# Grouped attention with SwiGLU on one core: who reads the fourth head's scores out of PSUM, and in how many exponentials

## The chip, the cores and the metric

The kernel runs on one core of a Trainium2 chip. The time is device microseconds of one launch, the median of several runs. Instruction times come from one profiled execution. Engines: PE multiplies matrices into PSUM, VectorE (DVE) and ScalarE (ACT) read PSUM and write SBUF, GpSimd (POOL) works on SBUF only, SyncE (SP) issues DMAs.

## The reference, cut to what matters

Two layers, each an attention block and a feed-forward block, with normalised inputs and residual sums. The sequence has 2048 rows of 448; 16 query heads of width 28 share one key and one value head.

```python
def _A_ref(x, wq, wk, wv, wo):
    q = (x @ wq).reshape(B, S, H, Dh).transpose(0, 2, 1, 3)
    k = x @ wk
    v = x @ wv
    scores = einsum("bhqd,bkd->bhqk", q, k) * (Dh ** -0.5)
    o = einsum("bhqk,bkd->bhqd", softmax(scores), v)
    return o.transpose(0, 2, 1, 3).reshape(B, S, H * Dh) @ wo
...
x = x + _A_ref(_layernorm(x), A_wq, A_wk, A_wv, A_wo)
x = x + _B_ref(_layernorm(x), B_w_gate, B_w_up, B_w_down)   # (silu(x @ w_gate) * (x @ w_up)) @ w_down
# and both once more
```

## The kernel before, in words

Every engine runs its instructions in the order in which the program lists them (`manual_schedule`, line 73); semaphores between engines are set by the framework from the tiles that are written and read. So the order of the Python calls is each engine's queue.

**Attention, `scores` (line 565).** Queries are cut into 4 chunks of 512 rows and 4 groups of 4 heads: 16 groups i (`GR`). For each, 16 key tiles of 128 keys are walked through: 256 steps n a layer, two steps to a pair d. `step(n)` (line 595) multiplies key tile kt with the 4 heads of the group. The heads use 32 rows of PE each and run beside each other; three products (high and low parts of the numbers) add up for each head. Heads 0 to 2, the triples, go to `three`, three PSUM banks; there are two such sets, for even and odd steps. Head 3, the single, goes to `one`, one of the two other banks, 6 and 7: `single(n // 2 + n)` (line 572 and 599).

Then come the exponentials (lines 608 to 618). In an even step ScalarE takes the single straight from PSUM (line 616), then the triples (line 617). In an odd step it takes the triples first (line 611); VectorE copies the single to SBUF as `raw` (line 613), and ScalarE takes it from there (line 614).

`pv(d)` (line 640) multiplies the exponentials of a pair's two steps with the values. Its result goes to bank `single(d + 1)`, and VectorE adds it to the group's sums in SBUF (line 657; line 654 copies for a group's first pair). A bank of the singles so holds in turn an even step's single, the product of the pair before, and an odd step's single. The loop that sets the order stands in lines 708 to 733: for an odd n it calls `step(n)`, then `pv(d - 1)`, then `between(d)`, which three times a layer does the output projection of a chunk in the same banks (lines 630 to 638), then what is due of `post`.

`post(i)` (line 661) divides: a DMA takes the row sums (line 668), and `rest`, called three pairs later out of `due`, checks their range and takes reciprocals on VectorE (lines 674 to 676), sends them out and back by two DMAs on SP (lines 678, 679) and multiplies and splits on GpSimd (lines 686, 687). `later` holds the steps of the next normalisation, spread over single n (lines 693 to 706).

**Maxima.** A softmax needs a bound for each query. `diagonal` (line 392) writes `kdiag`, block-diagonal copies of eight keys; `maxima` (line 419) multiplies them with the queries and reduces on VectorE (lines 426 to 435). For the last chunk it runs after step 1 of the stage, in bank 6 (line 724).

**Buffers.** `halves(name)` (line 119) hands out two buffers of 128x1024 in turn, for the group's sums (`o2`), the feed-forward's hidden values (`h2`) and one weight load.

**Feed-forward** (line 751 on) isn't changed; its first unit follows the stage's last `pv` on PE (lines 734 to 737). The branch with `full=True` runs only if a range check fails, which doesn't happen here.

Of the kernel before, what the change touches and what calls it, by code (L numbers as in the profile page):

```python
# [8 lines left out]
F32 = mybir.dt.float32  # L9
F32R = mybir.dt.float32r  # L10
AF = mybir.ActivationFunctionType
# [4 lines left out]
P = 128  # L16
# [11 lines left out]
SCALE = DH ** -0.5  # L28
# [24 lines left out]
def forward(  # L53
# [14 lines left out]
    nc = tc.nc  # L68
# [9 lines left out]
    pers = ctx.enter_context(tc.tile_pool(name="pers", bufs=1))  # L78
# [40 lines left out]
    def halves(name):  # L119

        return pers.tile([P, 2, 512], F32R, tag="halves", name=name, bufs=2)
# [28 lines left out]
    qts = [pers.tile([P, 2, 512], F32R, name=f"qstack{n}") for n in range(2)]  # L150
    qraw = pers.tile([P, 512], F32, name="qraw")
    bottom = pers.tile([4, 32], F32, name="bottom")
    kd, mask = None, None
    if not full:
        kd, mask = pers.tile([P, 4, P], F32R, name="kdiag"), pers.tile([P, 16, 4], F32, name="mask")

    def weights(fc):
        fs = slice(P * fc, P * fc + P)
# [173 lines left out]
    class Attention:  # L332
# [58 lines left out]

        def diagonal(self):

            nc.vector.tensor_tensor(
                kd[0:112].rearrange("p g (n k) -> p (g n) k", k=8),
                self.few[0:112, None, :].to_broadcast([112, 64, 8]),
                mask[0:112].rearrange("p n j -> p (n j)")[:, :, None].to_broadcast([112, 64, 8]),
                ALU.mult,
            )
# [19 lines left out]
        def maxima(self, c, cands=ALL):  # L419


            pm = bank(cands)[1]
            for n, g in enumerate(TURN):
                nc.tensor.matmul(pm, kd[0:112, g, :], self.hi[g], start=(n == 0), stop=(n == 3))  # L424
            side = pers.tile([P, 512], F32, name="sg")
            nc.vector.transpose(side, pm)
            ng = pers.tile([P, 64], F32, name="ng")
            nc.vector.tensor_reduce(ng, side.rearrange("p (n k) -> p n k", k=8), AX.X, ALU.max, negate=True)
            two = pers.tile([P, 4, 2, 16], F32R, name="two")
            hi, lo = two[:, :, 0, :], two[:, :, 1, :]  # L430
            ng = ng.rearrange("p (b j) -> p j b", j=4)
            nc.vector.tensor_copy(hi, ng)
            nc.vector.tensor_tensor(lo, ng, hi, ALU.subtract)
            flat = pers.tile([P, P], F32, name="flat")
            nc.vector.transpose(flat, two.rearrange("p j z b -> p (j z b)").bitcast(F32))
            self.rowsof[c] = dram.tile([P, P], F32, name=f"rows{self.layer}_{c}")
            nc.sync.dma_start(self.rowsof[c], flat)
# [10 lines left out]
        def max_steps(self, i):  # L448

            got = {}  # L450
            q = qts[i % 2]

            def one(j, qt, kc):
                if not got:
                    got["mx"] = pers.tile([P, 16, KC], F32, name="mx", bufs=2)
                n = 4 * j + qt
                pm = self.mbank()[1]
                js, qs = slice(32 * j, 32 * j + 32), slice(P * qt, P * qt + P)
                for n_, (z, k) in enumerate(((0, 0), (1, 0), (0, 1))):
                    nc.tensor.matmul(  # L460
                        pm, q[js, z, qs], keys[kc][js, k, :], start=(n_ == 0), stop=(n_ == 2), tile_position=(32 * j, 0)
                    )
                nc.vector.tensor_reduce(got["mx"][:, n, kc : kc + 1], pm, AX.X, ALU.max)

            def fin():
                got["ng"] = pers.tile([P, 16], F32, name="ng", bufs=2)
                nc.vector.tensor_reduce(got["ng"], got["mx"], AX.X, ALU.max, negate=True)

            def place(pn=None):

                if pn is None:
                    pn = self.mbank()[1]
                nc.tensor.transpose(pn[0:16, 0:P], got["ng"], ident)
                nh = pers.tile([16, P], F32R, name="nh", bufs=2)
                nl = pers.tile([16, P], F32R, name="nl", bufs=2)
                nc.vector.tensor_copy(nh, pn[0:16, 0:P])
                nc.vector.tensor_tensor(nl, pn[0:16, 0:P], nh, ALU.subtract)
                for z, n_ in enumerate((nh, nl)):
                    dma(q[28:125:32, z, :].rearrange("j (t w) -> j t w", w=P), n_)

            order = [(j, qt, kc) for j in range(4) for qt in range(4) for kc in range(KC)]
            if i == 0:
                order.sort(key=lambda o: o[2])
            fs = [lambda o=o: one(*o) for o in order]
            return fs[:-1] + [lambda: (fs[-1](), fin())], place
# [79 lines left out]
        def scores(self, ff):  # L565
            next(switch)
            with tc.tile_pool(name=f"at{self.layer}", bufs=1, reuse_waits="tile") as wp:
                woh = wp.tile([P, NG, D], F32R, name="woh")
                wol = wp.tile([P, NG, D], F32R, name="wol")
                on, accs, pts = {}, {}, {}  # L570
                todo, due = [], {}
# [23 lines left out]
                def step(n):  # L595


                    i, kt = divmod(n, NT)
                    three, one = threes[n % 2], single(n // 2 + n)
                    q, k, ks = qts[i % 2], keys[kt // 4], slice(P * (kt % 4), P * (kt % 4) + P)  # L600
                    for z, (kp, part) in enumerate(((0, 0), (1, 0), (0, 1))):
                        for j in range(4):
                            js = slice(32 * j, 32 * j + 32)
                            nc.tensor.matmul(  # L604
                                three[:, j, :] if j < 3 else one, k[js, kp, ks], q[js, part, :],
                                start=(z == 0), stop=(z == 2), tile_position=(32 * j, 0),
                            )
                    pt = wp.tile([P, 3, 512], F32, name="pt", bufs=3)
                    pt1 = wp.tile([P, 512], F32, name="pt1", bufs=3)
                    if n % 2:  # L610
                        nc.scalar.activation(pt, three, AF.Exp, scale=SCALE)  # L611
                        raw = wp.tile([P, 512], F32, name="raw")
                        nc.vector.tensor_copy(raw, one)  # L613
                        nc.scalar.activation(pt1, raw, AF.Exp, scale=SCALE)  # L614
                    else:
                        nc.scalar.activation(pt1, one, AF.Exp, scale=SCALE)  # L616
                        nc.scalar.activation(pt, three, AF.Exp, scale=SCALE)  # L617
                    pts[n] = [*(pt[:, j, :] for j in range(3)), pt1]

                def between(d):  # L620

# [39 lines left out]
                def post(i):  # L661

                    c, g = GR[i]
                    out2 = accs.pop(i)
                    oraw, rb = out2[:, 0, :], out2[:, 1, :]
                    rs = wp.tile([P, 16], F32, name="rs", bufs=2)
                    for j in range(4):
                        nc.sync.dma_start(rs[32 * j : 32 * j + 32, :], oraw[32 * j + DH : 32 * j + DH + 1, :])

                    def rest():  # L670
                        if fine is not None:
                            under = wp.tile([P, 16], F32, name="under", bufs=2)
                            for bound, op in ((LIMIT, ALU.is_lt), (1.0 / LIMIT, ALU.is_gt)):
                                nc.vector.tensor_scalar(under, rs, bound, None, op)
                                nc.vector.tensor_tensor(fine, fine, under, ALU.mult)
                        nc.vector.reciprocal(rs, rs)
                        rd = dram.tile([4, 512], F32, name="rd", bufs=2)
                        nc.sync.dma_start(rd.rearrange("j (p n) -> (j p) n", n=16), rs)
                        nc.sync.dma_start(rb, rd[:, None, :].to_broadcast([4, 32, 512]))
                        if g == 0:  # L680
                            on[c] = (
                                wp.tile([P, NG, 512], F32R, name="onh"),
                                wp.tile([P, NG, 512], F32R, name="onl"),
                            )
                        oh, ol = on[c]
                        nc.gpsimd.tensor_tensor(rb, oraw, rb, ALU.mult)
                        split(oh[:, g, :], ol[:, g, :], rb)
                        if g == NG - 1 and c < NC - 1:
                            todo.append(c)

                    return rest
# [16 lines left out]
                for n in range(last):  # L708
# [17 lines left out]
                        later.pop(n)()  # L726
                    d, odd = divmod(n, 2)
                    if odd:
                        if d:
                            pv(d - 1)  # L730
                        between(d)
                        if d in due:
                            due.pop(d)()
                pv(last // 2 - 1)
                self.lent = None
                next(switch)
# [292 lines left out]
```

## Time and profile before

| | before |
|---|---|
| median of 3 runs | 1986.77 us (1986.52 to 1987.32) |
| span of the profiled execution, first to last instruction | 1984.8 us |
| mean granted PE clock | 0.999 |
| ScalarE rows in the stages: triples (lines 611 and 617), 256 each | 1454 and 1453 ns |
| ScalarE: single from SBUF (line 614), from PSUM (line 616), 256 each | 622 and 591 ns |
| VectorE: single's copy (line 613), 256; sum's add (line 657), 224 | 692 and 691 ns |
| PE: value matmuls (line 647), 4096 | 598 ns |

Beside its span the profiled execution has no time of its own on record; the median of the runs lies 2.0 us above the span. A row names the line, the engine, what it writes from what, how often, and the mean of one. Rows of a timeline begin with start and duration in us; brackets at the end give the idle time before and what ended it. Instructions on PE, VectorE and ScalarE overlap their neighbours a little, so durations add up to more than the distance of their starts.

### The profile page before, as it was taken

How to read it: one execution, taken by the hardware profiler on the slowest of the kernel's cores; microseconds unless marked ns; L12 is line 12 of the kernel's file. 1: busy time of each engine (PE TensorE's matmuls, PEld its weight loads, DVE VectorE, ACT ScalarE, POOL GpSimd, SP SyncE). 2: the span in 40 equal slices, each digit the busy share in tenths (PEclk: the TensorE clock that was granted, in tenths of full speed). 3: DMA queues.
4: the chain of work that ended last, by engine and by line, in shares of the span. 5: the costliest groups of instructions: out<-in, count | busy, mean ns of one | idle time of the engine just before them, and what ended most of it. 6: DMA issues, size and time to landing. Idle time of an engine off the chain costs nothing. (4 is left out here: it accounts for less than half of the span.)

```text
span 1984.8 us, 44687 instructions
## 1 busy us (share of the span) xinstructions
PE 1969.2 (99%) x18519; PEld 1322.9 (67%) x18519; DVE 812.1 (41%) x1410; ACT 1278.6 (64%) x2140; POOL 528.7 (27%) x571
## 2 busy tenths in 40 slices
PE   9999999999999999999999999999999999999998
PEld 7544545445458999999984444454454789988887
DVE  7444543544434222322554335445454432222222
ACT  4899797997953333333349998979979433333332
POOL 4212111132213233333341221111231232233320
PEclk9999999999999999999999999999999999999999
DMA  5101020121210011100131111102111101011102
GB/s 163 55 23 31 23 51 21 32 58 28 72 33 9 24 32 32 32 24 19 51 107 35 30 31 30 44 12 61 32 55 45 31 17 30 18 31 32 32 1 76
DMA packets 93382, 77.52 MB, mean 39 GB/s; under 512 B 23510, under 2 KB 76374, under 8 KB 93174
## 3 DMA queue, kind: packets, MB, share of 16 engines
q1 hardware_dynamic: 92886, 74.16, 13.5%
q8 instruction: 146, 2.39, 0.5%
q14 instruction: 62, 0.51, 0.1%
q10 hardware_dynamic: 288, 0.46, 0.1%
HBM read 55.06 MB, written 18.74 MB: 37 GB/s over the span
## 5 line engine op out<-in xcount | busy, mean ns | idle before, releaser
L647 PE MATMUL bank<-pt,vsb 128*32 128x512 f32 x4096 | 493.3, 598 | 0.5
L604 PE MATMUL bank<-qstack,keys 32*128 32x512 f32 x1536 | 484.2, 424 | 1.7 <-DVE xres L591 1.7
L604 PE MATMUL three<-qstack,keys 32*128 32x512 f32 x4608 | 461.4, 425 | 1.5 <-DVE vt L538 1.2
L604 PEld LDWEIGHTS three<-qstack,keys 32*128 32x128 f32 x4608 | 254.2, 182 | 295.0 <-ACT pt L617 181.1
L321 PE MATMUL bank<-xh,wgh 64*128 64x512 f32 x1728 | 437.5, 389 | 0.1
L611 ACT ACTIVATE pt<-three 128x1536 f32<-128x1536 f32 x256 | 372.2, 1454 | 0.6 <-ACT pt L617 0.3
L617 ACT ACTIVATE pt<-three 128x1536 f32<-128x1536 f32 x256 | 372.0, 1453 | 0.0
L321 PE MATMUL bank<-xh,wgl 64*128 64x512 f32 x1404 | 363.0, 390 | 0.0
L321 PE MATMUL bank<-wdh,h 64*128 64x448 f32 x1792 | 330.2, 364 | 1.4 <-ACT h L889 1.0
L321 PE MATMUL bank<-xl,wgh 64*128 64x512 f32 x1296 | 328.3, 389 | 0.0
L888 DVE TENSOR_TENSOR sg<-bank,sg 128x512 f32<-128x512 f32 x112 | 77.4, 691 | 497.6 <-ACT sg L887 488.4
L647 PEld LDWEIGHTS bank<-pt,vsb 128*32 128x32 f32 x4096 | 107.1, 109 | 250.2 <-issue 152.6
L613 DVE COPY raw<-bank 128x512 f32<-128x512 f32 x256 | 177.2, 692 | 230.7 <-PE bank L604 228.5
L321 PEld LDWEIGHTS bank<-xh,wgh 64*128 64x128 f32 x1728 | 256.9, 184 | 16.7 <-issue 0.9
L798 POOL TENSOR_TENSOR xres<-stage,xres 128x448 f32<-128x448 f32 x108 | 127.7, 1203 | 499.6 <-ACT stage L797 499.6
L657 DVE TENSOR_TENSOR o<-bank,o 128x512 f32<-128x512 f32 x224 | 154.9, 691 | 241.7 <-PE bank L647 237.1
L321 PEld LDWEIGHTS bank<-wdh,h 64*128 64x128 f32 x1792 | 240.5, 184 | 15.6 <-issue 2.0
L604 PEld LDWEIGHTS bank<-qstack,keys 32*128 32x128 f32 x1536 | 243.8, 183 | 4.6 <-DVE xres L591 3.6
L328 ACT COPY seen<-bank 128x1 f32<-128x1 f32 x664 | 81.0, 163 | 238.9 <-PE bank L321 236.4
L321 PEld LDWEIGHTS bank<-xh,wgl 64*128 64x128 f32 x1404 | 212.1, 184 | 13.8
L321 PE MATMUL bank<-wdl,h 64*128 64x448 f32 x896 | 215.6, 367 | 0.0
L887 ACT ACTIVATE sg<-bank 128x512 f32<-128x512 f32 x112 | 67.3, 601 | 223.2 <-PE bank L321 214.2
(127 smaller groups left out, 2259.3 us busy)
## 6 DMA issues: line engine op xcount, KB each, us to landing
o<-rd SPq DMA_DIRECT2D x32, 256.0 KB
qraw<-qd SPq DMA_DIRECT2D x128, 56.0 KB
qd<-stage SPq DMA_DIRECT2D x30, 224.0 KB
xt<-xn SPq DMA_DIRECT2D x28, 224.0 KB
wdr<-in_B_w_down_dram SPq DMA_DIRECT2D x28, 224.0 KB
xn<-xt SPq DMA_DIRECT2D x7, 768.0 KB
wr<-in_B_w_gate_dram SPq DMA_DIRECT2D x28, 192.0 KB
wr<-in_B_w_up_dram SPq DMA_DIRECT2D x28, 192.0 KB
```

Of the source, the lines that this page charges most:

```text
L321: nc.tensor.matmul(po, a, b, start=start, stop=stop, skip_group_check=True)
L328: nc.scalar.copy(seen[:, i : i + 1], po[:, 0:1])
L604: nc.tensor.matmul(three[:, j, :] if j < 3 else one, k[js, kp, ks], q[js, part, :], start=(z == 0), stop=(z == 2), tile_position=(32 * j, 0),)
L611: nc.scalar.activation(pt, three, AF.Exp, scale=SCALE)
L613: nc.vector.tensor_copy(raw, one)
L617: nc.scalar.activation(pt, three, AF.Exp, scale=SCALE)
L647: nc.tensor.matmul(po[32 * j : 32 * j + 32, :], vsb[:, n % NT, :], pts[n][j], start=(n == 2 * d), stop=(n > 2 * d), skip_group_check=True,)
L657: nc.vector.tensor_tensor(acc, in_turn(po), acc, ALU.add)
L798: nc.gpsimd.tensor_tensor(r, s, r, ALU.add)
L887: nc.scalar.activation(by_tile(sg), in_turn(pg[0]), AF.Silu)
L888: nc.vector.tensor_tensor(by_tile(sg), in_turn(pg[1]), by_tile(sg), ALU.mult)
```

## The change

VectorE now copies the singles of both steps of a pair into one 128x1024 tile `raw`, and after the odd step's triples ScalarE takes one exponential over both, in place. The triples' exponentials have four buffers instead of three, `raw` two; the separate single tiles are gone. What is due of `post` is called ahead of the value matmuls instead of behind `between`. `kdiag` no longer has a tile of its own but takes one of the `halves`, newly in each layer. Four small tiles (`nh`, `nl`, `rs`, `under`) have one buffer instead of two; the first two are used only in the branch that doesn't run.

```diff
@@ diagonal, maxima
-    kd, mask = None, None
-    if not full:
-        kd, mask = pers.tile([P, 4, P], F32R, name="kdiag"), pers.tile([P, 16, 4], F32, name="mask")
+    mask = None if full else pers.tile([P, 16, 4], F32, name="mask")
...
+            self.kd = halves("kdiag")[:, 0, :].rearrange("p (g k) -> p g k", g=4)
...
@@ step
-                    pt = wp.tile([P, 3, 512], F32, name="pt", bufs=3)
-                    pt1 = wp.tile([P, 512], F32, name="pt1", bufs=3)
+                    pt = wp.tile([P, 3, 512], F32, name="pt", bufs=4)
+                    if n % 2 == 0:
+                        self.raw = wp.tile([P, 2, 512], F32, name="raw", bufs=2)
+                    raw = self.raw
+                    nc.scalar.activation(pt, three, AF.Exp, scale=SCALE)
+                    nc.vector.tensor_copy(raw[:, n % 2, :], one)
                     if n % 2:
-                        nc.scalar.activation(pt, three, AF.Exp, scale=SCALE)
-                        raw = wp.tile([P, 512], F32, name="raw")
-                        nc.vector.tensor_copy(raw, one)
-                        nc.scalar.activation(pt1, raw, AF.Exp, scale=SCALE)
-                    else:
-                        nc.scalar.activation(pt1, one, AF.Exp, scale=SCALE)
-                        nc.scalar.activation(pt, three, AF.Exp, scale=SCALE)
-                    pts[n] = [*(pt[:, j, :] for j in range(3)), pt1]
+                        nc.scalar.activation(raw, raw, AF.Exp, scale=SCALE)
+                    pts[n] = [*(pt[:, j, :] for j in range(3)), raw[:, n % 2, :]]
@@ post
-                    rs = wp.tile([P, 16], F32, name="rs", bufs=2)
+                    rs = wp.tile([P, 16], F32, name="rs")
...
-                            under = wp.tile([P, 16], F32, name="under", bufs=2)
+                            under = wp.tile([P, 16], F32, name="under")
@@ the loop over the steps
                     if odd:
+                        if d in due:
+                            due.pop(d)()
                         if d:
                             pv(d - 1)
                         between(d)
-                        if d in due:
-                            due.pop(d)()
```

More of the change, by code (lines that the diff above doesn't have):

```diff
@@ L392, in diagonal @@
         def diagonal(self):
+            self.kd = halves("kdiag")[:, 0, :].rearrange("p (g k) -> p g k", g=4)
             nc.vector.tensor_tensor(
-                kd[0:112].rearrange("p g (n k) -> p (g n) k", k=8),
+                self.kd[0:112].rearrange("p g (n k) -> p (g n) k", k=8),
                 self.few[0:112, None, :].to_broadcast([112, 64, 8]),
@@ L423, in maxima @@
             for n, g in enumerate(TURN):
-                nc.tensor.matmul(pm, kd[0:112, g, :], self.hi[g], start=(n == 0), stop=(n == 3))
+                nc.tensor.matmul(pm, self.kd[0:112, g, :], self.hi[g], start=(n == 0), stop=(n == 3))
             side = pers.tile([P, 512], F32, name="sg")
@@ L473, in place @@
                 nc.tensor.transpose(pn[0:16, 0:P], got["ng"], ident)
-                nh = pers.tile([16, P], F32R, name="nh", bufs=2)
-                nl = pers.tile([16, P], F32R, name="nl", bufs=2)
+                nh = pers.tile([16, P], F32R, name="nh")
+                nl = pers.tile([16, P], F32R, name="nl")
                 nc.vector.tensor_copy(nh, pn[0:16, 0:P])
```

## The prediction, made before the changed kernel was run

> **What bounds the kernel now.** I start from the page's busy line and from the windows of the two attention stages, because the change touches almost nothing outside them. The window columns are start:end, length, then the busy time of PE, weight load, VectorE, ScalarE and GpSimd, and last the granted clock, the DMA share and GB/s.
>
> ```profile
> PE 1969.2 (99%) x18519; PEld 1322.9 (67%) x18519; DVE 812.1 (41%) x1410; ACT 1278.6 (64%) x2140; POOL 528.7 (27%) x571
> 65.00:571.00 506.00, 504.17 (x5255) 226.52 (x5256) 230.22 (x413) 473.87 (x513) 109.15 (x111) 1.00 0.14 36
> 1047.00:1553.00 506.00, 504.15 (x5260) 226.44 (x5256) 229.53 (x413) 474.17 (x513) 109.70 (x111) 1.00 0.14 36
> ```
>
> The granted clock is 1.00 in both, so the clock explains nothing. PE is "busy" for 504 of 506 us, but its weight loads fill only 226 us, so this is no proof of a saturated PE: matmuls that stand beside each other or wait count too. ScalarE is busy for 474 us of 506. I therefore look at one pair of key tiles (steps 2d and 2d+1), first on ScalarE:
>
> ```profile
> 1235.56 1.46 ACT L617 ACTIVATE pt<-three 128x1536 f32<-128x1536 f32 x1
> 1236.90 1.45 ACT L611 ACTIVATE pt<-three 128x1536 f32<-128x1536 f32 x1
> 1238.25 0.62 ACT L614 ACTIVATE pt<-raw 128x512 f32<-128x512 f32 x1
> 1238.77 0.59 ACT L616 ACTIVATE pt<-bank 128x512 f32<-128x512 f32 x1
> 1239.25 1.45 ACT L617 ACTIVATE pt<-three 128x1536 f32<-128x1536 f32 x1
> ```
>
> Start to start these take 1.34, 1.35, 0.52 and 0.48, together 3.69 us, and each starts before the one ahead of it has ended. ScalarE has no gap: **its ring is 3.69 us for a pair**. A layer has 128 pairs, two layers 256.
>
> Then the same pair on PE and VectorE. P is the start of a pair's first value matmul (line 647).
>
> ```profile
> 1235.73 1.92 PE L647 MATMUL bank<-pt,vsb 128*32 128x512 f32 x16
> 1237.59 0.49 PE L604 MATMUL bank<-qstack,keys 32*128 32x512 f32 x1
> 1238.15 0.39 PE L604 MATMUL bank<-qstack,keys 32*128 32x512 f32 x1
> 1238.52 0.50 PE L604 MATMUL bank<-qstack,keys 32*128 32x512 f32 x1
> 1239.09 0.39 PE L604 MATMUL bank<-qstack,keys 32*128 32x512 f32 x1
> 1239.41 1.92 PE L647 MATMUL bank<-pt,vsb 128*32 128x512 f32 x16
> ```
>
> ```profile
> 1237.77 0.69 DVE L657 TENSOR_TENSOR o<-bank,o 128x512 f32<-128x512 f32 x1 [1.19 <-PE bank L647]
> 1239.59 0.69 DVE L613 COPY raw<-bank 128x512 f32<-128x512 f32 x1 [1.12 <-PE bank L604]
> ```
>
> Three matmuls write each single (head 3 of the four); shown are the first and last for each of the two steps. The next P comes 3.68 after this one, and here too every hop is filled. The add of line 657 starts at P+2.04 and ends at P+2.73. It frees the bank that the odd step's single goes to, and that single starts at P+2.79, 0.06 after the add. Its last matmul starts 0.57 later and the next value matmul 0.32 after that. Is that 0.32 PE's own, or a wait for line 616, which ends at 1239.36? A pair in which the add came late tells:
>
> ```profile
> 407.24 0.69 DVE L657 TENSOR_TENSOR o<-bank,o 128x512 f32<-128x512 f32 x1 [1.54 <-PE bank L647]
> 407.88 0.59 ACT L616 ACTIVATE pt<-bank 128x512 f32<-128x512 f32 x1
> 407.98 0.18 PEld L604 LDWEIGHTS bank<-qstack,keys 32*128 32x128 f32 x1 [0.28 <-DVE o L657]
> 408.55 0.39 PE L604 MATMUL bank<-qstack,keys 32*128 32x512 f32 x1
> 408.87 0.16 PEld L647 LDWEIGHTS bank<-pt,vsb 128*32 128x32 f32 x8 [0.37 <-ACT pt L616]
> ```
>
> Line 616 had ended at 408.47, 0.40 before the value matmuls began; what they followed was the late single, again by 0.57 + 0.32. So there is a second ring without ScalarE: 2.04 + 0.69 + 0.06 + 0.57 + 0.32 = **3.68 us**. The kernel stands on two rings of the same length, and a shorter one alone buys nothing.
>
> **The change, part by part.**
>
> *One exponential for both singles.* Gone is a whole instruction with its fixed part; the 1024 elements stay. No 128x1024 exponential is in the trace. The nearest read from SBUF are these two:
>
> ```profile
> L193 ACT CAST wh<-wr 128x896 fp32r<-128x896 f32 x1 | 0.9, 939 | 8.1 <-DMA wr<-in_A_wq_dram 8.1
> L614 ACT ACTIVATE pt<-raw 128x512 f32<-128x512 f32 x256 | 159.3, 622 | 0.0
> ```
>
> They differ by 317 ns for 384 elements, 0.83 ns each, so 1024 elements take about 939 + 106 = 1045 ns. Line 614 is followed after 0.52 of its 0.62, so 0.10 comes off: 0.95 us. A lower end is the elements alone, 1024 x 0.83 = 0.85; an upper end two reads as now, 1.04. I take 0.95, next to both rows. ScalarE's ring becomes 1.34 + 1.35 + 0.95 = 3.64 (bounds 3.54 to 3.73): 0.05 per pair, 12.8 us in all, if nothing else held.
>
> *The even single goes through VectorE.* The value matmuls of pair d-1 write the bank that held the even single of pair d, so they wait for whoever reads it. That was line 616 (0.59), now it is a copy like line 613 (0.69). By the pair above: the even single's last matmul starts at P+2.42, and line 613 starts 0.50 after such a matmul (1239.09 to 1239.59), so at P+2.92; the add ahead of it in VectorE's queue ended at P+2.73. It ends at P+3.61, and 0.05 later PE goes on: P+3.66. This third ring is 3.66, under the add's 3.68 by a hair, over ScalarE's new 3.64. **So the period stays 3.68**, and the 0.05 turns into idle time of ScalarE. I take nothing for the steady pairs (from -0.04 to +0.04 each, -10 to +10 us). The page "VectorE: DVE Perf Modes" of the Trainium skill, Specifications, says that VectorE sits closer to SBUF and ScalarE closer to PSUM. By that rule this move of a PSUM read is the wrong way round; the trace agrees, with 0.69 against 0.59.
>
> *Start of each stage.* The singles' copies now stand in VectorE's queue, and the last maxima (line 724) are queued ahead of the copy of step 2.
>
> ```profile
> 1047.71 0.43 DVE L527 CAST q<-sg 112x512 fp32r<-112x512 f32 x1
> 1049.90 0.72 DVE L426 STREAM_TRANSPOSE sg<-bank 128x512 f32<-128x512 f32 x1 [0.41 <-PE bank L424]
> 1052.16 0.65 DVE L613 COPY raw<-bank 128x512 f32<-128x512 f32 x1
> ```
>
> ```profile
> 1048.64 1.20 PE L424 MATMUL bank<-q,kdiag 112*128 112x512 f32 x4
> 1051.57 1.92 PE L647 MATMUL bank<-pt,vsb 128*32 128x512 f32 x16
> ```
>
> The copy of step 0 comes after line 527: 1048.06 to 1048.75. It frees bank 6 for the maxima's matmuls, which then start at 1048.80 instead of 1048.64. The maxima's VectorE work takes 2.26 (1049.90 to 1052.16) and now ends at 1052.32; the copy of step 2 follows to 1053.01, and the first value matmuls start at 1053.06 instead of 1051.57. That is 1.5 us late, and the PE ring, which has no slack, doesn't win it back: **3.0 us** for two layers. Bounds: nothing, and the whole block with a copy, 2.9 per layer.
>
> *Output projection inside the stage* (line 638, three times a layer). Behind it the ring restarts:
>
> ```profile
> 1197.65 0.39 PE L604 MATMUL bank<-qstack,keys 32*128 32x512 f32 x1
> 1198.12 0.60 ACT L616 ACTIVATE pt<-bank 128x512 f32<-128x512 f32 x1 [10.47 <-PE bank L604]
> 1198.77 1.92 PE L647 MATMUL bank<-pt,vsb 128*32 128x512 f32 x16
> ```
>
> The copy would run from 1198.15 to 1198.84 and PE go on at 1198.89, 0.12 later; six times, **0.7 us**.
>
> *End of each stage.* The last value matmuls wait for the last exponential of the singles.
>
> ```profile
> 1549.20 4.25 PE L647 MATMUL bank<-pt,vsb 128*32 128x512 f32 x32
> 1551.72 0.62 ACT L614 ACTIVATE pt<-raw 128x512 f32<-128x512 f32 x1
> 1553.37 0.50 PE L301 MATMUL bank<-xh,wgh 128*128 128x512 f32 x1
> ```
>
> Now only the odd tile's single is late, and line 301 follows 1.03 after it (1552.34). Afterwards both are late: the wide exponential ends about P+2.98 with P = 1549.20 (triples at P-0.75 and P+0.59, singles at P+1.94), and two singles, one behind the other on the same columns, take about 0.9 more than one: 1552.18 + 1.9 = 1554.1, 0.7 late; two layers, **1.4 us** (bounds 0 and 1.8).
>
> *The division's VectorE work moves ahead of the value matmuls* (lines 732 and 733 to ahead of 729).
>
> ```profile
> 1216.23 0.17 DVE L674 TENSOR_SCALAR under<-rs 128x16 f32<-128x16 f32 x1
> 1217.11 1.01 DVE L239 STREAM_TRANSPOSE xn<-sg 128x448 f32<-128x448 f32 x1
> 385.42 2.46 SPq L668 DMA_DIRECT2D rs<-o  x4
> 390.26 0.69 DVE L613 COPY raw<-bank 128x512 f32<-128x512 f32 x1 [1.13 <-PE bank L604]
> ```
>
> It holds VectorE for 0.88. In its new place it follows the odd step's copy (P+3.36+0.50 = P+3.86 to P+4.5) and ends at P+5.4, ahead of the next add at P+5.7, so it is hidden by the value matmuls. Its input, the four DMAs of line 668, was issued by 387.88 and is wanted 0.61 after the copy at 390.26: 3.0 us, which I take as enough; its two DMAs on SP's queue only come earlier. In six groups a normalisation step and in four a cast and a subtraction (0.4 to 0.7 each) stand in the same pair; there the add comes about 0.08 and 0.24 late: 6 x 0.08 + 4 x 0.24 = **1.5 us**.
>
> *Four buffers of triples, two of singles, fewer of the small tiles.* The line 611 wait on value matmuls goes, but ScalarE has slack now anyway. The maxima's keys in a sums' buffer: their writer (line 394, 0.69, once a layer) could wait for the down matmuls of an earlier unit; those stand ahead of the projection on PE, so I take 0, and 1 us a layer without that cover.
>
> **Sum.** The span is 1984.8; the median of the runs, 1986.77, lies 2.0 above it, and I add to the median: 0 + 3.0 + 0.7 + 1.4 + 1.5 = 6.6, so **1993.4 us**, 0.33% slower. My own range for this case is 1989 to 1998.
>
> **Rivals.** *ScalarE alone sets the period* (the other side: faster). For it: no gap on ScalarE. Against it: the pair at 407. It decides if the add ring and the copy ring come out under 3.64, which needs the 0.32 before the value matmuls or the 0.50 before the copy to shrink by 0.04. Then 256 x 0.05 = 12.8 goes: 1986.8 + 6.6 - 12.8 = 1980.6. The page "Perfetto Trace Analysis" of the Trainium skill, Identifying the Most-Contended Engine, says to improve the engine with the highest occupancy first; in the stage that is ScalarE (474 of 506), and by this rule the change would give this rival's time.
>
> *The single costs are absorbed*: the start and the end are hidden by work I don't see, and the period stays. About 1986 to 1990, say 1988.
>
> *The VectorE ring grows*: the copy of the even single and the add, now one behind the other, each wait a little more, 0.04 a pair. 1993.4 + 256 x 0.04 = 2003.6. Nothing in the rows asks for it, but 0.02 of slack is little. *The wide exponential isn't shorter* (1.04): ScalarE's ring is 3.73 and the time about the same, 2005.
>
> **Chances.** Forecast 0.58, absorbed costs 0.22, ScalarE alone 0.12, the last two 0.08. A measurement of this kernel can tell about 0.2%, 4 us, from no change. A small part of the forecast's own range (under 1990.7, 0.09) lies within that: same 0.22 + 0.09 = 0.31, faster 0.12, slower 0.49 + 0.08 = 0.57. The range is 1982 to 2000: it takes in the forecast, the absorbed costs and the nearer half of the steady pairs' bounds, and leaves out most of the faster rival and the last two.
>
> **What the changed profile would show.** The exponential of the singles near 1.05 us, 256 of them; a pair's ScalarE rows adding up to 3.64 with a small gap ahead of the triples; P to P still 3.68; value matmuls waiting for VectorE's copy or following the single by 0.32; the first value matmuls 1.5 later after the stage's first exponential; line 301 behind the stage 0.7 later. I am wrong if P to P is 3.64 or less (the rings through VectorE are shorter than read) or 3.72 and more (they are longer), or if the extra waits at the two ends are missing.

## The result, and the profile after

| | before | after |
|---|---|---|
| median | 1986.64 us (1986.46 to 1987.32, 4 runs) | 1996.07 us (1996.0 to 1996.79, 4 runs) |
| span of the profiled execution | 1984.8 us | 1994.3 us |
| first score matmul to first value matmul, second layer | 5.41 us | 6.95 us |
| median pair, P to P | 3.69 us | 3.72 us |
| pair that holds an output projection | 14.26 us | 14.37 us |
| 127th of the stage's 128 Ps to the feed-forward's first matmul | 4.17 us | 4.83 us |

The changed kernel is slower: ratio 1.005, 95% interval 1.0038 to 1.0062, 9.4 us. The granted clock is 0.999 in both.

The page of the changed kernel, busy line first, then ScalarE's and VectorE's groups in the stage (line 611 is the triples' exponential, 612 the copy of a single, 614 the exponential over both singles):

```profile
PE 1971.9 (99%) x18519; PEld 1343.5 (67%) x18519; DVE 984.9 (49%) x1666; ACT 1283.6 (64%) x1884; POOL 528.7 (27%) x571
...
L611 ACT ACTIVATE pt<-three 128x1536 f32<-128x1536 f32 x512 | 715.0, 1448 | 68.6 <-PE three L603 63.0
...
L612 DVE COPY raw<-bank 128x512 f32<-128x512 f32 x512 | 354.3, 693 | 89.7 <-ACT raw L614 63.4
```

The change does what it says: 512 copies where there were 256, and 256 fewer instructions on ScalarE. What one wide exponential costs, and what ended PE's waits ahead of the value matmuls, stands in the views by form and by waits:

```profile
L614 ACT ACTIVATE raw<-raw 128x1024 f32<-128x1024 f32 x256 | 271.9, 1062 | 0.0
```

```profile
PEld bank L644 <- DVE raw L612: 116.2, 254, 1.7
```

The same view of the kernel before:

```profile
PEld bank L647 <- ACT pt L616: 94.7, 254, 0.6
```

The columns of the waits are the sum in us, how many, and the longest. 254 times, in nearly all of the 256 pairs, the value matmuls now go when VectorE's copy has ended, where they went when ScalarE's line 616 had. So the copy is what ends last in a pair. One pair shows it, on PE, VectorE and ScalarE (the even step's single ends with the row at 1237.96, the odd step's are those at 1238.26 to 1238.83):

```profile
1235.52 0.63 PE L644 MATMUL bank<-pt,vsb 128*32 128x512 f32 x3
1237.94 0.40 PE L603 MATMUL three<-qstack,keys 32*128 32x512 f32 x3
1237.96 0.39 PE L603 MATMUL bank<-qstack,keys 32*128 32x512 f32 x1
1238.26 0.49 PE L603 MATMUL bank<-qstack,keys 32*128 32x512 f32 x1
1238.83 0.39 PE L603 MATMUL bank<-qstack,keys 32*128 32x512 f32 x1
1239.23 0.63 PE L644 MATMUL bank<-pt,vsb 128*32 128x512 f32 x3
```

```profile
1237.51 0.69 DVE L654 TENSOR_TENSOR o<-bank,o 128x512 f32<-128x512 f32 x1 [0.53 <-PE bank L644]
1238.49 1.46 DVE L612 COPY raw<-bank 128x512 f32<-128x512 f32 x2 [0.28 <-ACT raw L614]
```

```profile
1234.73 2.79 ACT L611 ACTIVATE pt<-three 128x1536 f32<-128x1536 f32 x2 [0.43 <-PE three L603]
1237.41 1.06 ACT L614 ACTIVATE raw<-raw 128x1024 f32<-128x1024 f32 x1
1238.44 2.79 ACT L611 ACTIVATE pt<-three 128x1536 f32<-128x1536 f32 x2
```

With P = 1235.52, the even single's last matmul starts at P+2.44, the copy 0.53 after it, and the next value matmul 0.74 after the copy's start. The medians over 239 pairs are 2.43, 0.54 and 0.75, together 3.72. The add ring had room: the add starts at P+1.99 and the odd single follows; its last matmul, 1238.83, would have let the value matmuls go 0.32 later, at 1239.15. They went at 1239.23. ScalarE had room as well: from the wide exponential to the next triples it takes 1.03 where 0.95 was forecast, because it waits for the triples. (Where it waits less, in the run with half of the copy below, the median of this step is 0.95.)

The trace's semaphore records, which the views don't list, show what the copy waits for. PE's signal for the even single comes 0.444 after the start of the single's last matmul. VectorE has its wait for PE in a semaphore instruction ahead of the copy. That instruction starts 0.027 after the signal, and the copy 0.065 after it. Over the 239 pairs these last two spread by 0.002 or less, so neither a buffer nor ScalarE holds the copy.

Two places outside the pairs. The start of the second layer's stage, PE first (the step's scores, the maxima's keys of line 423, the first value matmuls), then VectorE (lines 425 to 434 are the maxima):

```profile
1050.22 0.51 PE L603 MATMUL three<-qstack,keys 32*128 32x512 f32 x3
...
1052.97 1.19 PE L423 MATMUL bank<-q,kdiag 112*128 112x512 f32 x4 [0.21 <-DVE raw L612]
...
1057.17 0.63 PE L644 MATMUL bank<-pt,vsb 128*32 128x512 f32 x3 [1.23 <-DVE raw L612]
```

```profile
1052.23 1.31 DVE L612 COPY raw<-bank 128x512 f32<-128x512 f32 x2
1054.20 0.72 DVE L425 STREAM_TRANSPOSE sg<-bank 128x512 f32<-128x512 f32 x1 [0.67 <-PE bank L423]
...
1056.23 0.31 DVE L434 STREAM_TRANSPOSE flat<-two 128x128 f32<-128x128 f32 x1
1056.46 1.25 DVE L612 COPY raw<-bank 128x512 f32<-128x512 f32 x2
```

The copy of step 2 is the first of the two at 1056.46, behind the maxima, and PE waited 1.23 for it. And the end of the stage:

```profile
1558.03 0.63 PE L644 MATMUL bank<-pt,vsb 128*32 128x512 f32 x3
...
1561.03 0.62 PE L644 MATMUL bank<-raw,vsb 128*32 128x512 f32 x1 [0.22 <-ACT raw L614]
...
1562.86 0.50 PE L299 MATMUL bank<-xh,wgh 128*128 128x512 f32 x1
```

Here the two last singles stand alone behind the wide exponential, and the feed-forward follows 4.83 after P (1558.03, the 127th of the stage's 128) instead of 4.17.

**Where the 9.5 us of span went**, in the second layer: start 6.95 - 5.41 = 1.54; from the first P to the 127th 500.86 - 497.63 = 3.23; end 4.83 - 4.17 = 0.66; together 5.4. The first layer has 1.46, 3.18 and 0.66, together 5.3. Two layers make 10.7, and the work ahead of the first layer's stage was 1.3 shorter in this profile. It varies by itself: the first score matmul came at 64.01 us before and at 62.69 here, and between 63.4 and 66.0 in the profiles of the changed kernel's variants below.

### The profile page after: what moved, and what is told of

It reads as the page before. It is cut to its first block, busy times and chain, and to the rows that moved or that the text cites. A ratio compares the mean times of both kernels' runs of the same rounds, so it can differ in the third digit from the quotient of the medians.

```text
span 1994.3 us, 44611 instructions
## 1 busy us (share of the span) xinstructions
PE 1971.9 (99%) x18519; PEld 1343.5 (67%) x18519; DVE 984.9 (49%) x1666; ACT 1283.6 (64%) x1884; POOL 528.7 (27%) x571
## 5 line engine op out<-in xcount | busy, mean ns | idle before, releaser
L611 ACT ACTIVATE pt<-three 128x1536 f32<-128x1536 f32 x512 | 715.0, 1448 | 68.6 <-PE three L603 63.0
L644 PE MATMUL bank<-raw,vsb 128*32 128x512 f32 x1024 | 487.4, 598 | 0.4 <-ACT raw L614 0.4
L603 PE MATMUL bank<-qstack,keys 32*128 32x512 f32 x1536 | 470.6, 424 | 2.4 <-DVE xres L590 1.7
L603 PE MATMUL three<-qstack,keys 32*128 32x512 f32 x4608 | 430.3, 408 | 1.2 <-DVE vt L537 1.2
L603 PEld LDWEIGHTS three<-qstack,keys 32*128 32x128 f32 x4608 | 261.9, 183 | 230.6 <-issue 189.4
L612 DVE COPY raw<-bank 128x512 f32<-128x512 f32 x512 | 354.3, 693 | 89.7 <-ACT raw L614 63.4
L644 PEld LDWEIGHTS bank<-pt,vsb 128*32 128x32 f32 x3072 | 101.7, 109 | 269.4 <-issue 153.2
L614 ACT ACTIVATE raw<-raw 128x1024 f32<-128x1024 f32 x256 | 271.9, 1062 | 0.0
```

The lines of the kernel that those rows point to most:

```text
L603: nc.tensor.matmul(three[:, j, :] if j < 3 else one, k[js, kp, ks], q[js, part, :], start=(z == 0), stop=(z == 2), tile_position=(32 * j, 0),)
L612: nc.vector.tensor_copy(raw[:, n % 2, :], one)
L614: nc.scalar.activation(raw, raw, AF.Exp, scale=SCALE)
L644: nc.tensor.matmul(po[32 * j : 32 * j + 32, :], vsb[:, n % NT, :], pts[n][j], start=(n == 2 * d), stop=(n > 2 * d), skip_group_check=True,)
```

## The experiments: which ring sets the period

Two theories were open. **Copy ring**: the period is 3.72 because the even single's last matmul, VectorE's copy and PE's next value matmuls form a ring, and the copy comes 0.54 instead of 0.50 after the matmul. **Rivals**: ScalarE's wide exponential, the copy's buffers, or the add.

*The single issued first.* The four heads' score matmuls of a part go to four row strips of PE. In the changed kernel the single, head 3, is the fourth of them.

```diff
-                        for j in range(4):
+                        for j in (3, 0, 1, 2):
```

> The changed kernel with the heads of a step issued in the order 3, 0, 1, 2 instead of 0, 1, 2, 3, nothing left out. Copy-ring theory: the last matmul of the single is the first of its four instead of the fourth, so the copy starts 0.02 to 0.05 earlier, the period falls from 3.72 to 3.67 to 3.70, and the time by 5 to 12 us to 1984 to 1991. If the late start of the copy (0.53 after the matmul, where 0.50 was read before) has another cause than the place among the four, such as ScalarE or a second wait, nothing changes: 1996.

Measured: 1986.37 us (10 runs), ratio to the kernel before 0.9999 (0.9989 to 1.0009); span 1984.6; median pair 3.67. The total is that of the kernel before again: pairs shorter by 0.02 than its 3.69 pay for the two ends, which stay late (6.97 at the start of the second layer's stage, 4.92 at the end). A pair, with P = 1229.08:

```profile
1229.08 0.63 PE L644 MATMUL bank<-pt,vsb 128*32 128x512 f32 x3
1231.50 0.39 PE L603 MATMUL bank<-qstack,keys 32*128 32x512 f32 x1
1232.75 0.63 PE L644 MATMUL bank<-pt,vsb 128*32 128x512 f32 x3
```

```profile
1232.00 1.51 DVE L612 COPY raw<-bank 128x512 f32<-128x512 f32 x2 [0.23 <-PE three L603]
```

```profile
1231.06 1.06 ACT L614 ACTIVATE raw<-raw 128x1024 f32<-128x1024 f32 x1
```

The matmul starts at P+2.42 as ever; the copy follows by 0.50 instead of 0.54, and PE 0.75 after that: 3.67. By the semaphore records the 0.04 lies in PE's signal. PE signals the triples and the single one after the other. Issued fourth, the single has the second signal, 0.444 after its last matmul's start; issued first, it has the first, at 0.406. What follows the signal is the same in both (0.027 and 0.065). This also settles a misleading row. In the changed kernel the profile puts the copy's wait down to line 614 (63.4 us of 89.7). Here the copy starts at 1232.00, before the wide exponential of that time has ended (1231.06 + 1.06 = 1232.12). It isn't waiting for it; in the changed kernel the two only fell together.

*The same edit in the kernel before.*

> The kernel before with the heads issued in the order 3, 0, 1, 2; nothing left out. There ScalarE's ring (3.69) has no gap, so an earlier single is worth nothing: 1985 to 1987.5, period 3.69. If the kernel before were held by the ring through VectorE and PE, the single's earlier place would shorten the period by 0.03 to 0.1 and the time by 8 to 25 us.

Measured: 1989.45 us (10 runs), ratio 1.0016 (1.0007 to 1.0026); median pair 3.70. No gain, and over the expected range. There ScalarE reads the even single, and VectorE's copy of it isn't in a ring. So the order of issue helps only where VectorE's copy is what ends last. The kept traces show where the 3 us come from. The odd step's single has to wait for the bank that the add frees. Issued first, it keeps its step's triples waiting behind it: these start at P+2.79 instead of P+2.68 (medians). The step's last matmul then starts at P+3.379 instead of P+3.365, and the next value matmul follows by 0.32 in both. That is 0.013 a pair.

*Half of the even single's copy.* Two fixed `raw` tiles, cleared at the start of each stage, and 256 columns instead of 512. The other half of the even single keeps old numbers.

```diff
+                raws = [wp.tile([P, 2, 512], F32, name=f"raw{n}") for n in range(2)]
+                for r in raws:
+                    nc.gpsimd.memset(r, 0.0)
...
-                    nc.vector.tensor_copy(raw[:, n % 2, :], one)
+                    w = 512 if n % 2 else 256
+                    nc.vector.tensor_copy(raw[:, n % 2, 0:w], one[:, 0:w])
```

> The changed kernel, but VectorE copies only 256 of the 512 columns of each even step's single (the other half keeps old numbers, so that part of the attention isn't computed). Copy-ring theory (value matmuls, even step, copy, value matmuls set the period of 3.72): the copy falls from 0.69 to about 0.43, that ring to 3.46, and the period to what ScalarE allows, 3.64 to 3.66; the time falls by 256 x 0.06 = 15 us to about 1981. ScalarE theory (the wide exponential makes ScalarE's own ring 3.72): no change, 1996. Add-ring theory (the sums' add still sets the period): no change, 1996.

Measured: 2000.57 us in one run, span 1998.8, so the total is a miss; the period is 3.63. The total says nothing on the ring, because the clearing stands in GpSimd's queue behind other work and holds up the start of each stage by 12 us (19.0 and 18.9 from the first score matmul to the first value matmul, where the changed kernel has 6.95):

```profile
76.02 1.84 POOL L574 MEMSET raw<- 128x1024 f32 x2
77.01 1.02 DVE L614 COPY raw<-bank 128x256 f32<-128x256 f32 x2 [11.67 <-POOL raw L574]
```

Between the Ps the reading is clean. Three starts of value matmuls, and one of the copies between them:

```profile
1234.91 0.63 PE L646 MATMUL bank<-pt,vsb 128*32 128x512 f32 x3
...
1238.55 0.63 PE L646 MATMUL bank<-pt,vsb 128*32 128x512 f32 x3
...
1242.18 0.63 PE L646 MATMUL bank<-pt,vsb 128*32 128x512 f32 x3
```

```profile
1237.89 0.42 DVE L614 COPY raw<-bank 128x256 f32<-128x256 f32 x1 [0.29 <-PE three L606]
```

A copy shorter by 0.27 shortens the pair by 0.09, to 3.64 and 3.63, and then something else holds. That is the length that the add ring (2.74 + 0.57 + 0.32 = 3.63) and ScalarE's (1.35 + 1.33 + 0.95 = 3.63 by the medians of this run) both have; the run doesn't tell them apart. From the first P to the 127th the two stages are 10.2 and 10.4 shorter than in the changed kernel.

*ScalarE relieved.* The even single isn't exponentiated at all; the exponential runs over the odd one alone, and VectorE's pass stays.

```diff
-                    nc.vector.tensor_copy(raw[:, n % 2, :], one)
                     if n % 2:
-                        nc.scalar.activation(raw, raw, AF.Exp, scale=SCALE)
+                        nc.vector.tensor_copy(raw[:, 1, :], one)
+                    else:
+                        nc.vector.tensor_scalar(raw[:, 0, :], one, 0.0, 1.0, ALU.mult, ALU.add)
+                    if n % 2:
+                        nc.scalar.activation(raw[:, 1, :], raw[:, 1, :], AF.Exp, scale=SCALE)
```

> The changed kernel, but the exponential takes only the odd step's single (512 elements instead of 1024); VectorE's copy of the even single is an operation of the same size that writes ones, so the even tile's fourth head isn't computed. Copy-ring theory: period stays 3.72 in the steady pairs, because ScalarE isn't in the ring; only the end of each stage gains a little, so 1994 to 1996. ScalarE theory: ScalarE's ring falls by 0.43 and the period to the next ring, 3.63 to 3.68, so 1973 to 1986.

Measured: 1995.46 us in one run, span 1993.7, period 3.72 as before the edit. The window of the second stage (the fourth busy time is ScalarE's):

```profile
1053.00:1559.00 506.00, 503.05 (x5216) 231.98 (x5220) 313.58 (x538) 420.03 (x381) 107.74 (x105) 1.00 0.13 35
```

ScalarE is busy for 52 us less than the changed kernel's 472 in the same window and has 86 of 506 to spare, and the pair isn't shorter by anything. ScalarE is out of the ring.

*All of the change but the exponentials.* The singles are treated as in the kernel before; the division's place, the buffers and the keys' tile are as in the changed kernel.

```diff
+                    pt1 = wp.tile([P, 512], F32, name="pt1", bufs=3)
                     if n % 2:
+                        nc.scalar.activation(pt, three, AF.Exp, scale=SCALE)
+                        raw = wp.tile([P, 512], F32, name="raw")
+                        nc.vector.tensor_copy(raw, one)
+                        nc.scalar.activation(pt1, raw, AF.Exp, scale=SCALE)
+                    else:
+                        nc.scalar.activation(pt1, one, AF.Exp, scale=SCALE)
+                        nc.scalar.activation(pt, three, AF.Exp, scale=SCALE)
```

> The changed kernel with the exponentials and the singles' copies of the kernel before (straight from PSUM in even steps, by way of VectorE in odd ones), and all the rest of the change: four buffers of triples, keys of the maxima in a sums' buffer, single buffers of the small tiles, the division's work ahead of the value matmuls. Copy-ring theory: the rest is worth nothing, 1986 to 1988, period 3.69. Rival (the moved division or the shared buffer costs the time): 1990 to 1996.

Measured: 1985.73 us (10 runs), ratio 0.9998 (0.9988 to 1.0007); period 3.68; the start of the second stage takes 5.38. The four buffers, the shared tile and the moved division are worth nothing here, and the loss is in the singles alone.

*The division behind `between` again.*

```diff
                     if odd:
-                        if d in due:
-                            due.pop(d)()
                         if d:
                             pv(d - 1)
                         between(d)
+                        if d in due:
+                            due.pop(d)()
```

> The changed kernel with what is due of the division back in its old place, behind the value matmuls and the sums' add; nothing left out. Copy-ring theory: its 0.88 us of VectorE work then stands between the add and the even single's copy, and the copy starts at P+3.5 instead of P+2.97 in one pair of each group: 0.5 to 0.65 for 30 groups, 16 to 20 us, so 2012 to 2016, with periods of 4.25 to 4.4 once in eight pairs. If VectorE's queue isn't in the ring: 1996.

Measured: 2009.74 us in one run, 13.7 over the changed kernel and under the 2012 to 2016 that were expected. Fifteen pairs of each layer now take 4.15 instead of 3.72, and 30 x 0.43 = 13. One of them on VectorE:

```profile
1160.53 0.69 DVE L654 TENSOR_TENSOR o<-bank,o 128x512 f32<-128x512 f32 x1 [1.23 <-PE bank L644]
1161.14 0.17 DVE L671 TENSOR_SCALAR under<-rs 128x16 f32<-128x16 f32 x1
...
1161.85 0.24 DVE L673 RECIPROCAL rs<-rs 128x16 f32<-128x16 f32 x1
1162.01 1.22 DVE L612 COPY raw<-bank 128x512 f32<-128x512 f32 x2
```

The division stands between the add and the copy, where VectorE had idled about 0.28, and the copy starts at P+3.47 (P = 1158.54) instead of P+2.97. VectorE is busy for 49% of the span, and still 0.9 us in that place delays PE by half of it. The moved division is thus no part of the loss but a need of the new copy.

## The experiments: the two ends of a stage, and a faster version

*The maxima one step later.*

```diff
-                    if not full and n == 1:
+                    if not full and n == 2:
```

> The changed kernel with the last maxima called after step 2 of a stage instead of after step 1, so that the copy of step 2's single stands ahead of them in VectorE's queue; nothing left out. If the start of the stage costs what the trace shows (first value matmuls 1.5 us later in each layer) and the ring can't win it back, the time falls by about 3 us to 1993, and the first value matmuls start about 5.5 us after step 0's first matmul instead of 6.95. If the ring had won it back anyway, or the copy of step 3 now comes late instead: 1996.

Measured: 1997.56 us (4 runs), ratio 1.0055 (1.004 to 1.0071), period 3.72. A miss: 3 us were to come off, and from the first score matmul (1052.24) to the first value matmul it takes 7.16 instead of 6.95. VectorE and PE:

```profile
1057.74 0.72 DVE L425 STREAM_TRANSPOSE sg<-bank 128x512 f32<-128x512 f32 x1 [0.44 <-PE bank L423]
...
1060.00 0.65 DVE L612 COPY raw<-bank 128x512 f32<-128x512 f32 x1
```

```profile
1058.52 0.49 PE L603 MATMUL bank<-qstack,keys 32*128 32x512 f32 x1 [0.38 <-DVE sg L425]
...
1059.08 0.39 PE L603 MATMUL bank<-qstack,keys 32*128 32x512 f32 x1
1059.40 0.63 PE L644 MATMUL bank<-pt,vsb 128*32 128x512 f32 x3
```

The wait only changed its name. Step 3's single now waits for the maxima's PSUM bank, which line 425 frees, and the value matmuls follow that single's last matmul by 0.32.

*The single first, the maxima one step later, and two separate exponentials in the last two steps.*

```diff
-                        for j in range(4):
+                        for j in (3, 0, 1, 2):
...
-                    if n % 2:
+                    if n >= NT * len(GR) - 2:
+                        nc.scalar.activation(raw[:, n % 2, :], raw[:, n % 2, :], AF.Exp, scale=SCALE)
+                    elif n % 2:
...
-                    if not full and n == 1:
+                    if not full and n == 2:
```

> The changed kernel with three edits: heads in the order 3, 0, 1, 2; the last maxima after step 2; in a stage's last two steps one exponential for each single. Nothing left out. Period 3.67 as in the first edit alone (1986.4), less 3 us at the starts and about 1.3 at the ends: 1982, faster than both. If the gains don't add up: 1985 to 1987.

Measured: 1984.67 us (11 runs), ratio 0.9995 (0.9986 to 1.0004). The start takes 7.17, again no gain from the maxima; the end takes 4.15 (1547.70 to 1551.85), down from 4.92 with the single first. Two such ends are 1.5, about the 1.7 by which this median lies below that of the run with the single first.

*The edges as before.* The first two pairs and the last pair of each stage treat the singles as the kernel before does, so that step 2 needs nothing of VectorE while the maxima hold it.

```diff
-                    nc.scalar.activation(pt, three, AF.Exp, scale=SCALE)
-                    nc.vector.tensor_copy(raw[:, n % 2, :], one)
+                    ends = n < 4 or n >= NT * len(GR) - 2
+                    if ends and n % 2 == 0:
+                        nc.scalar.activation(raw[:, 0, :], one, AF.Exp, scale=SCALE)
+                    nc.scalar.activation(pt, three, AF.Exp, scale=SCALE)
+                    if n % 2 or not ends:
+                        nc.vector.tensor_copy(raw[:, n % 2, :], one)
                     if n % 2:
-                        nc.scalar.activation(raw, raw, AF.Exp, scale=SCALE)
+                        z = raw[:, 1, :] if ends else raw
+                        nc.scalar.activation(z, z, AF.Exp, scale=SCALE)
```

> The changed kernel, but in the first two pairs and in the last pair of each attention stage the singles are treated as in the kernel before: ScalarE reads the even single itself, two separate exponentials. Measured so far: each stage starts 1.5 us late and ends 0.66 us late by the change; putting the maxima one step later took nothing off the start, because the maxima's 2.26 us of VectorE work then stood ahead of the copy of step 3 instead. Theory (what costs at the start is that the even single of step 2 needs VectorE while VectorE is held by the maxima): the first value matmuls come 5.4 us after the stage's first score matmul instead of 6.95, the end goes from 4.83 back to 4.17, the period stays 3.72: 1996.1 - 2 x 1.5 - 2 x 0.66 = about 1991.8. Rival (the start is late because the copy of step 0 pushes the maxima's matmuls, and the later work of the stage absorbs part of it): 1994 to 1996.

Measured: 1992.45 us (7 runs), ratio 1.003 (1.0018 to 1.0041), 3.6 below the changed kernel. In the second layer the start takes 5.38 (1048.54 to 1053.92) and the end 4.13 (1555.78 to 1559.91); the period stays 3.72.

*The edges as before, and the single first.* Both edits, nothing else.

> The same edges (first two pairs and last pair of a stage as in the kernel before) and the single issued first among the four heads of a step, so that the period is 3.67. Theory (start, end and period add up): 1986.4, the time with the single first, less 2 x 1.5 and 2 x 0.75, about 1982, 0.2% under the kernel before. Rival (as for the run with the edges alone, the edges give nothing): 1985 to 1986.5.

Measured: 1981.0 us (8 runs), ratio to the kernel before 0.9973 (0.9963 to 0.9984): **faster than both kernels**. The start on PE and on VectorE:

```profile
1044.78 0.50 PE L603 MATMUL bank<-qstack,keys 32*128 32x512 f32 x1
...
1050.19 0.63 PE L649 MATMUL bank<-pt,vsb 128*32 128x512 f32 x3
```

```profile
1049.27 0.69 DVE L427 TENSOR_REDUCE ng<-sg 128x64 f32<-128x512 f32 x1
...
1050.79 0.65 DVE L616 COPY raw<-bank 128x512 f32<-128x512 f32 x1
```

The first value matmuls come 5.41 after the first score matmul, while VectorE is still at the maxima and before its copy of step 3 has begun. The end takes 4.11 (1546.65 to 1550.76), the median pair 3.67.

## Why the prediction was right, and where it was not

The forecast of 1993.4 us lies 2.7 under the measured 1996.07, inside its own range of 1989 to 1998, with the sign right. But P to P is 3.72, which the prediction had named as a sign that it is wrong ("3.72 and more": the rings through VectorE are longer than read). On the steady pairs it was wrong. By stages the change costs 10.7 us where 6.6 was forecast; the 1.3 by which the work ahead of the first stage was shorter brought the total nearer, and that was luck. Step by step:

- **The wide exponential**, forecast 1045 ns and 0.95 as a step on ScalarE: measured 1062 ns. ScalarE got its gap, and it bought nothing, which the run with ScalarE relieved shows. The rule of the Trainium skill's page "Perfetto Trace Analysis", Identifying the Most-Contended Engine, to take the engine with the highest occupancy first, leads here to ScalarE and so to the rival's 1980.6. The trace doesn't agree: ScalarE's share was 474 of 506, relieving it bought nothing, and the time rose by 9.4.
- **The steady pairs, forecast at 0: this is the step that was mis-sized.** The prediction put the third ring at P+3.66, "under the add's 3.68 by a hair". The third ring was there as described, the numbers on both sides were not. The 0.50 from the single's last matmul to the copy was read after an *odd* step, whose single runs later than its triples; the *even* single runs beside its triples and the copy comes 0.54 after it. So the ring is 2.43 + 0.54 + 0.75 = 3.72. The add ring didn't stay at 3.68 either: the add now starts at P+1.99 instead of P+2.05, so it would have allowed 3.63. By the semaphore records PE's signal for it comes 0.637 after the start of the last value matmul in both kernels. Before, a semaphore instruction stood between the signal and the add, which started 0.08 after the signal; now the add waits for PE itself and starts after 0.02. The price is 0.03 a pair at the median; the second layer's stretch of 3.23 less three output projections of 0.11 leaves 2.9 with the crowded pairs in it, about 5.8 us in two layers. That lies within the bounds given (-10 to +10), at neither end. The 0.69 against 0.59, which the prediction sets beside the move to VectorE, compares two engines at two operations and doesn't show where an engine sits; the ring grew ahead of the copy, which takes 0.69 as before.
- **Start of each stage**, forecast 1.5: measured 1.54, and for the reason given, since treating the first pairs as before brings it back to 5.38 and 5.41.
- **End of each stage**, forecast 0.7: measured 0.66; with the last pair treated as before the end takes 4.13 and 4.11. The "about 0.9" for a second single had no row behind it, but its sum held: from the last single's matmuls to the feed-forward it takes 1.83 (1561.03 to 1562.86), forecast 1.9.
- **Output projection**, forecast 0.12 each: measured 14.37 - 14.26 = 0.11.
- **The moved division**, forecast hidden but for 1.5 us in crowded pairs: mostly right. The crowded pairs that show take 3.84 or 3.85, 0.12 over their neighbours, two a layer: 0.5 us. Three other pairs, at 366, 370 and 1228 us, take 4.07, 4.34 and 4.18. In all three a normalisation step stands in VectorE's queue, and the copy starts at P+3.15 to P+3.33. In the two longest the step's line 232 runs for 1.39 and 1.23 and holds up the add, where in the third it takes 0.54. The three lose 1.4 us that no term of the sum has, though the kernel before has late pairs of about the same sum elsewhere. That the move keeps the division out of the copy's way, worth 13.7, was not in the prediction at all.
- **The buffers and the shared tile**, forecast 0: all of the change but the exponentials measures 1985.73, no different from before.

Of the rivals, "the VectorE ring grows" (0.04 a pair, 2003.6) named the ring that grew, by 0.03. Its reason, that copy and add delay each other, is not what happened: VectorE stands idle for 0.28 between them, and the copy is late because PE's signal is. It was given little chance for "nothing in the rows asks for it". A row did ask for care: line 616 and line 613 of the kernel before read singles of different steps, and only one of the two could be carried over. "ScalarE alone sets the period" needed the 0.50 to shrink by 0.04; instead it grew by as much, and only issuing the single first moved it back.

What stays open: why PE's second signal comes 0.03 after the first, and why line 232 takes 0.54 in one pair and 1.39 in another.

## What to carry to other kernels

Where an engine without gaps is relieved, write down every ring through the buffers with its length before counting the relief as gain; here three rings lay within 0.1 us of each other, and the one through a half-idle engine won. A delay from a producer to its reader has to be read on the same step, with the same neighbours, as the one that will use it. Work moved to another engine should leave out the steps in which that engine is held up by something else: the same edit that lost 0.5% as it was made won 0.27% with its edges left as they were and the producer issued first.

## What was not expected of the hardware

The time from the start of an even single's last score matmul to the start of VectorE's copy depends on its place among the four matmuls on the row strips, though the profile's modelled duration is 0.39 each time: 0.54 when it is issued fourth beside three others, 0.50 when it is issued first. It also depends on how the copy waits. Behind an output projection in the changed kernel it is 0.43, as for the copies of the odd steps (median 0.43):

```profile
1204.16 0.39 PE L603 MATMUL bank<-qstack,keys 32*128 32x512 f32 x1
```

```profile
1204.59 1.40 DVE L612 COPY raw<-bank 128x512 f32<-128x512 f32 x2 [1.05 <-PE bank L603]
```

These copies wait for PE alone and start 0.02 after its signal. The other even copies, and those of the kernel before, have a semaphore instruction of their own between the signal and the copy and start 0.09 after it. Since matmul ends are modelled, only the signals and the reader's start show this. In a ring that repeats 256 times, the 0.04 us of the place is most of the 9.7 us between the changed kernel and the one with the single first.
